# A two-layer attention and MLP training step: five wq chunks kept, w1's place lent to other loads, w2's chunks closed one by one

## The chip, the core and the metric

The kernel runs on one core of one Trainium2 chip. The metric is the device time of one execution in microseconds (us). Every matrix of weights is bf16 and far larger than what the core can keep, so it is moved in chunks of about 1 MB from HBM into the core's memory; results go back the same way.

## The reference

The forward pass is attention, MLP, attention, MLP on one token, with the same weights in both layers, and then the gradients of everything with respect to one given output gradient.

```python
def _A_ref(x, k_cache, v_cache, wq, wo):          # D=1024, 32 heads of 128, 4 kv heads, window W=4096
    q = (x @ wq).reshape(B, Sq, Hq, Dh) ...
    scores = jnp.einsum("bhqd,bhkd->bhqk", q, k) * (Dh ** -0.5)
    o = jnp.einsum("bhqk,bhkd->bhqd", _softmax(scores, axis=-1), v)
    return o... @ wo
def _B_ref(x, w1, b1, w2):                        # F=3584
    h = jnp.einsum("bsd,df->bsf", x, w1) + b1
    act = h * jnp.tanh(softplus(h))
    return jnp.einsum("bsf,fd->bsd", act, w2)
x = x + _A_ref(_layernorm(x), ...); x = x + _B_ref(_layernorm(x), ...)   # twice
...
_out, _vjp = jax.vjp(_f, A_x, A_k_cache, A_v_cache, A_wq, A_wo, B_w1, B_b1, B_w2)
return (_out0, *_vjp(grad_out))
```

The gradients of the two caches are as large as the caches (32768 rows, of which 4096 are in the window); all rows outside the window are zeros that must be written: 58.7 MB.

## The kernel before, in words

**The places in memory.** KT and VS hold the K and V windows of the four kv heads. W1 holds the whole of w1 (8 rows of chunks of 3584 columns). `ring_t` has 8 slots of 4096 columns; chunks of wq (8), wo (8) and w2 (7) pass through them. A chunk of wq, wo or w2 is 1 MB, one of w1 896 KB.

**The order of loads.** `Ring` (L38) holds a list of wanted loads, written out once at the start (L251 to L270): K into four ring slots, wq, V, two chunks of w2, wo, w1, the other five of w2, then for layer 1 wq, wo, and for the backward pass wq, w2, wo, wq again. `pump` (L51) issues from the head of the list on SP's queue as long as a slot is free; `release` (L77) frees a slot and pumps. Since this is done while the program is written down, the order of SP's queue is fixed; on the chip each load waits for the last reader or writer of its slot, and for the load eight places before it on the queue. SP also carries small moves of rows inside the core (L733, L737, L957, L792, L987) and the stores of the weights' gradients (L967, L972).

**Kept chunks.** `KEEP_Q = (6, 7)`: these wq chunks of layer 0 stay in their slots for layer 1, and six are loaded again. `KEEP_Q2 = (5, 6, 7)`: these stay after the backward pass of layer 1's attention (there already transposed in place, which `turned_q` remembers) for that of layer 0, and five are loaded again.

**Zero stores.** `zeros(n, after)` (L240) issues n stores of 1 MB of zeros on POOL's queue behind a one-element copy that waits for `after`. The 56 stores are dealt out over the milestones of the computation.

**The stages.** Forward: K transposes (L561), q (L473), scores, softmax, o, wo (L553), w1 (L601), w2 (`mlp_out`, L649). Since the output gradient is given, the product of w2's rows with it (da1) is made in the forward pass of layer 0, while w2 is in memory. `rows_chunk` (L447) does this: of a chunk's four row blocks two are dotted on VectorE (`rowdot`), and two are transposed on TensorE, copied back over the chunk by ScalarE and multiplied (`turned`, L427). The multiplication lags two blocks behind the transposes (`later`, `behind`), and the slot is released when it is done. For the last w2 chunk of layer 0 this is put off to `last_da` (L710), which attention of layer 1 calls ahead of its q. Backward: layer 1's MLP (`dn_b1`), layer 1's attention (`attn_bwd`, a loop over wo's chunks, scores, a loop over wq's chunks), layer 0's MLP (L1077 to L1081, forward product of layer 1's w2 and da0 together, then `dn_b0`), layer 0's attention. Last come the gradients of the weights and caches as outer products (L989 on), evacuated by ScalarE and VectorE into staging slots and stored. The staging slots are, in this order of taking, VS, KT, the ring and three slots at the end of W1.

Of the kernel before, what the change touches and what calls it, by code (L numbers as in the profile page):

```python
# [10 lines left out]
BF16 = mybir.dt.bfloat16  # L11
# [4 lines left out]
P = 128  # L16
HQ = 32
DH = 128
D = 1024
J = 4096  # L20
F = 3584
# [16 lines left out]
class Ring:  # L38
# [6 lines left out]
        self.pending = deque()  # L45
        self.where = {}

    def want(self, key, src, shape, own=None):
        self.pending.append((key, src, shape, own))

    def pump(self):  # L51
        while self.pending:
            key, src, shape, own = self.pending[0]
            if own is None:
                if not self.free:
                    return
                s = self.free.popleft()
                n = 1
                for k in shape[1:]:
                    n *= k  # L60
                dst = self.slots[s][:, 0:n]
                if len(shape) == 3:
                    dst = dst.rearrange("p (a b) -> p a b", a=shape[1])
                self.where[key] = (s, dst)
            else:
                dst = own
            self.pending.popleft()
            self.nc.sync.dma_start(dst, src)

# [6 lines left out]

    def release(self, key):  # L77
        s, _ = self.where.pop(key)
        self.free.append(s)
        self.pump()  # L80


# [1 line left out]
def kernel(  # L84
# [128 lines left out]
    def kv_src(cache, g):  # L213
        return cache[0, g, ZR:, :].rearrange("(p t) d -> p t d", p=P)
# [2 lines left out]
        for t in ts:  # L217
            ring.want(("q", k, t), wq_v[:, t, :], [P, J])

    def want_o(k, cs=range(8)):  # L220
        for c in cs:
            ring.want(("o", k, c), wo_v[:, c], [P, 4, D])

    def want_2(k, cs=range(7)):
        for c in cs:
# [22 lines left out]
                nc.gpsimd.dma_start(dst, zt[:])  # L248


    KEEP_Q = (6, 7)  # L251
    KEEP_Q2 = (5, 6, 7)
    EARLY_2 = (0, 1)
    for g in range(G):
        ring.want(("K", g), kv_src(A_k_cache, g), [P, TS, P])
    want_q(0)
    for g in range(G):
        ring.want(("V", g), kv_src(A_v_cache, g), None, own=VS[:, g])
    want_2(0, EARLY_2)
    want_o(0)  # L260
    for t in range(TD):
        ring.want(("1", t), w1_v[:, t, :], None, own=W1[:, t, :])
    want_2(0, [c for c in range(7) if c not in EARLY_2])
    want_q(1, [t for t in range(8) if t not in KEEP_Q])
    want_o(1)
# [161 lines left out]
    def turned(w, n, mv, eng=None, block=None):  # L427

        b = big().bitcast(BF16)
        for i in range(n):  # L430
            nc.tensor.transpose(b[:, i * P:(i + 1) * P], block(w, i) if block else w[:, i * P:(i + 1) * P], ident_bf[:])  # L431
        evac(w, b[:, 0:n * P], eng, cost=(0.69 * n / 8, n / 8))
        later(mv, True)
# [7 lines left out]
    def mv(w, n, out, rhs_of, last):  # L441
        for i in range(n):
            nc.tensor.matmul(out, lhsT=w[:, i * P:(i + 1) * P], rhs=rhs_of(i), start=fresh[0], stop=last and i == n - 1,  # L443
                             skip_group_check=True)
            fresh[0] = False

    def rows_chunk(ch, c, col, l, vec, dst, off, nr=2, eng="A"):  # L447

        for tt in range(4):
            r = 4 * c + tt  # L450
            if tt < nr:
                rowdot(ch[:, tt, :], [vec], D, dst[:, r:r + 1])
            else:
                w = ch[:, tt, :]
                turned(w, TD, lambda w=w, r=r: mv(w, TD, TP[:, off + r:off + r + 1], lambda i: col[:, i, l:l + 1], True), eng)

    def rows_join(dst, n, off):
        v = dst[:, 0:n].rearrange("p (a b) -> p a b", b=4)[:, :, 2:4]
# [136 lines left out]
    def mlp_fwd(l, x, st):  # L595
        name = f"B{l}"
        n32, rstd = ln_fwd(x, st, NB[:, :, l], name)
        h_ps = MV[:, 192:192 + TF]
        for t in range(TD):
            for fb in range(TF):  # L600
                nc.tensor.matmul(h_ps[:, fb:fb + 1], lhsT=f_block(W1[:, t], fb), rhs=NB[:, t, l:l + 1],  # L601
                                 start=(t == 0 and fb == 0), stop=(t == TD - 1), skip_group_check=True)
# [24 lines left out]
        if l == 0:  # L627
            V.tensor_tensor(out=AC[:, :, l], in0=h[:], in1=t_[:], op=ALU.mult)

        def deriv():  # L630

            mp, sg, s2 = col("mp"), col("sg"), col("s2")
            V.tensor_scalar(out=s2[:], in0=z[:], scalar1=1.0, scalar2=None, op0=ALU.add)
            V.reciprocal(s2[:], s2[:])
            V.tensor_tensor(out=sg[:], in0=m[:], in1=z[:], op=ALU.max)
            V.tensor_tensor(out=sg[:], in0=sg[:], in1=s2[:], op=ALU.mult)
            V.tensor_tensor(out=mp[:], in0=t_[:], in1=t_[:], op=ALU.mult)
            V.tensor_scalar(out=mp[:], in0=mp[:], scalar1=-1.0, scalar2=1.0, op0=ALU.mult, op1=ALU.add)
            V.tensor_tensor(out=mp[:], in0=mp[:], in1=h[:], op=ALU.mult)
            V.tensor_tensor(out=mp[:], in0=mp[:], in1=sg[:], op=ALU.mult)  # L640
            V.tensor_tensor(out=mp[:], in0=mp[:], in1=t_[:], op=ALU.add)
            return mp

        def act_late():
            V.tensor_tensor(out=AC[:, :, l], in0=h[:], in1=t_[:], op=ALU.mult)

        return dict(n32=n32, rstd=rstd, deriv=deriv, act_late=act_late)

    def mlp_out(l, ch, c, y_ps):  # L649
        for tt in range(4):  # L650
# [41 lines left out]
            early_da(2 * c + 1)  # L692

    x1, st1, sA0 = attn_fwd(0, x0, st0, True, wo_hook0)
    sB0 = mlp_fwd(0, x1, st1)
    mp0 = sB0["deriv"]()
    y_ps = MV[:, 256:256 + TD]
    mv_open()
    for c in range(7):
        ch = ring.get(("2", 0, c))  # L700
        mlp_out(0, ch, c, y_ps)
        if c in EARLY_2:
            ring.release(("2", 0, c))
        elif c < 6:
            rows_chunk(ch, c, GB, 1, gbc, da1, DA)
            later(lambda c=c: ring.release(("2", 0, c)))
    x2, st2 = residual(y_ps, x1, "B0")


# [223 lines left out]
                  dict(do=lambda c: conv(2), dp=dp3, dq=dq3, dn=dn3))  # L933


    W1S = W1[:].rearrange("p t f -> p (t f)")
    ROWS = W1S[:, 0:5120]
    NOFF = 1024
    rf = W1S[0:7, 5120:6144]
# [3 lines left out]
    DOST = W1S[:, 11008:11264]  # L943

    TWIN = W1S[:, 11264:16384]
    stage_free = deque(W1S[:, 16384 + i * SLOT:16384 + (i + 1) * SLOT] for i in range(3))
    rt_n = [0]

    def rowize(cols, n, base, off):
# [237 lines left out]
```

## Time and profile before

| what | us |
|---|---|
| median of 3 runs (lowest, highest) | 461.44 (459.64, 462.82) |
| span of the profiled execution | 460.6 |
| PE busy / PEld busy | 337.2 / 275.3 |
| DVE busy / ACT busy | 261.3 / 228.2 |
| DMA: loads and stores on SP's queue | 123.94 MB, 67.0% of 16 engines' span |
| DMA: zero stores on POOL's queue | 58.72 MB, 30.7% of 16 engines' span |

The page gives the span of one execution, from its first to its last instruction; it names no other time of its own, so the 0.84 us by which the median stands above it are taken as what lies around. PE is TensorE's matmuls, PEld its weight loads, DVE VectorE, ACT ScalarE, POOL GpSimd, SP the engine that issues most DMAs; a "q" behind a name (SPq) is the engine's sequencer. In the slices, each digit is the busy share of one fortieth of the span in tenths, and PEclk is TensorE's granted clock in tenths of full speed. A line of waits names who waited, for what, the us in total, the number of waits and the longest. A line of a timeline has start, duration, engine, line, operation, output and input, and in brackets the idle time of the engine ahead of it with what ended it.

### The profile page before, as it was taken

How to read it: one execution, taken by the hardware profiler on the slowest of the kernel's cores; microseconds unless marked ns; L12 is line 12 of the kernel's file. 1: busy time of each engine (PE TensorE's matmuls, PEld its weight loads, DVE VectorE, ACT ScalarE, POOL GpSimd, SP SyncE). 2: the span in 40 equal slices, each digit the busy share in tenths (PEclk: the TensorE clock that was granted, in tenths of full speed). 3: DMA queues.
4: the chain of work that ended last, by engine and by line, in shares of the span. 5: the costliest groups of instructions: out<-in, count | busy, mean ns of one | idle time of the engine just before them, and what ended most of it. 6: DMA issues, size and time to landing. Idle time of an engine off the chain costs nothing. (4 is left out here: it accounts for less than half of the span.)

```text
span 460.6 us, 14273 instructions
## 1 busy us (share of the span) xinstructions
PE 337.2 (73%) x6385; PEld 275.3 (60%) x6385; DVE 261.3 (57%) x517; ACT 228.2 (50%) x263; POOL 38.6 (8%) x85
## 2 busy tenths in 40 slices
PE   4836435597678788599879898897896876677950
PEld 3736435497668787599779898787791121112530
DVE  6505731383150149678428786475485987878860
ACT  2502001064035369378128573283267988778850
POOL 4000000000111320100210101102111000000000
PEclk9955555555555569799559855597595555555555
DMA  8999999999999999999999999979999999999995
GB/s 340 420 419 419 419 420 416 422 388 392 393 422 424 418 414 414 406 384 386 376 424 334 407 387 371 414 264 408 424 420 421 419 425 421 427 424 419 408 407 227
DMA packets 28379, 183.59 MB, mean 399 GB/s; under 512 B 3706, under 2 KB 3734, under 8 KB 9494
## 3 DMA queue, kind: packets, MB, share of 16 engines
q1 hardware_dynamic: 20162, 123.94, 67.0%
q0 software_dynamic: 8064, 58.72, 30.7%
q8 instruction: 50, 0.82, 0.7%
q14 instruction: 11, 0.09, 0.0%
q10 hardware_dynamic: 92, 0.02, 0.0%
HBM read 83.94 MB, written 98.62 MB: 396 GB/s over the span
## 5 line engine op out<-in xcount | busy, mean ns | idle before, releaser
L287 ACT COPY ring<-BIG 128x1024 bf16<-128x1024 bf16 x73 | 72.2, 1013 | 40.4 <-PE BIG L431 37.7
L431 PE MATMUL BIG<-ident_bf,ring 128*128 128x128 bf16 x872 | 80.0, 252 | 3.8 <-DMA ring<-in_A_wo_dram 2.0
L431 PEld LDWEIGHTS <-ring 128*128 128x128 bf16 x952 | 69.8, 114 | 5.2 <-DMA ring<-in_A_wo_dram 2.3
L995 PE MATMUL wide<-W 2*128 2x512 bf16 x228 | 48.5, 601 | 19.0 <-DVE ring L284 3.6
L408 DVE CUSTOM_DVE_ANT_0 junk<-ring,SC 128x1024 bf16<-128x1024 bf16 x38 | 46.2, 1216 | 4.5 <-DMA ring<-in_A_wo_dram 1.7
L995 PEld LDWEIGHTS <-W 2*128 2x128 bf16 x240 | 10.9, 103 | 54.5 <-issue 53.8
L443 PEld LDWEIGHTS <-ring 128*128 128x128 bf16 x1024 | 38.2, 100 | 4.6 <-ACT ring L287 4.4
L287 ACT COPY KT<-BIG 128x1024 bf16<-128x1024 bf16 x22 | 21.8, 1015 | 32.3 <-PE BIG L582 30.9
L287 ACT CAST ring<-wide 128x1024 bf16<-128x1024 f32 (+1 forms) x38 | 35.2, 998 | 4.9 <-PE wide L995 4.0
L284 DVE COPY ring<-BIG 128x1024 bf16<-128x1024 bf16 x36 | 24.8, 691 | 20.3 <-PE BIG L431 13.1
L284 DVE CAST ring<-wide 128x1024 bf16<-128x1024 f32 (+1 forms) x26 | 30.2, 1200 | 5.7 <-PE wide L995 5.2
L248 POOL DMA_DIRECT2D out_dram<-zt x56 | 29.6, 534 | 6.3 <-DMA out_dram<-zt 5.6
L553 PE MATMUL MV<-OC,ring 128*128 128x1 bf16 x512 | 16.6, 166 | 15.2 <-DMA ring<-in_A_wo_dram 12.6
L287 ACT COPY W<-BIG 128x1024 bf16<-128x1024 bf16 x20 | 18.9, 1151 | 15.7 <-PE BIG L766 15.7
L553 PEld LDWEIGHTS <-ring 128*128 128x128 bf16 x512 | 16.0, 106 | 16.0 <-DMA ring<-in_A_wo_dram 13.2
L284 DVE CAST VS<-wide 128x1024 bf16<-128x1024 f32 (+1 forms) x18 | 21.0, 1190 | 4.1 <-PE wide L995 3.1
L473 PE MATMUL MV<-NA,ring 128*128 128x1 bf16 x512 | 15.0, 165 | 10.9 <-DMA ring<-in_A_wq_dram 10.0
L601 PE MATMUL MV<-NB,W 128*128 128x1 bf16 x448 | 16.2, 172 | 9.2 <-DMA W<-in_B_w_dram 6.5
L408 DVE CUSTOM_DVE_ANT_0 junk<-ring,DSX 128x1024 bf16<-128x1024 bf16 x18 | 22.0, 1224 | 0.6
L601 PEld LDWEIGHTS <-W 128*128 128x128 bf16 x448 | 15.9, 118 | 9.8 <-DMA W<-in_B_w_dram 7.2
L1046 PE MATMUL wide<-W 32*128 32x256 bf16 x128 | 20.4, 403 | 1.4 <-ACT W L287 0.8
L473 PEld LDWEIGHTS <-ring 128*128 128x128 bf16 x512 | 14.3, 103 | 11.6 <-DMA ring<-in_A_wq_dram 10.6
(256 smaller groups left out, 539.1 us busy)
## 6 DMA issues: line engine op xcount, KB each, us to landing
out_dram<-zt POOLq DMA_DIRECT2D x56, 1024.0 KB, 12.7
ring<-in_A_wq_dram SPq DMA_DIRECT2D x27, 1024.0 KB
ring<-in_A_wo_dram SPq DMA_DIRECT2D x24, 1024.0 KB
ring<-in_B_w_dram SPq DMA_DIRECT2D x14, 1024.0 KB
out_dram<-ring SPq DMA_DIRECT2D x9, 1024.0 KB
W<-in_B_w_dram SPq DMA_DIRECT2D x8, 896.0 KB
ring<-in_A_k_cache_dram SPq DMA_DIRECT2D x4, 1024.0 KB
VS<-in_A_v_cache_dram SPq DMA_DIRECT2D x4, 1024.0 KB
```

Source lines behind the costliest of these rows:

```text
L248: nc.gpsimd.dma_start(dst, zt[:])
L284: nc.vector.tensor_copy(dst, src)
L287: nc.scalar.copy(dst, src)
L408: nc.vector.tensor_tensor_reduce(out=out, in0=a, in1=vec, scale=1.0, scalar=acc if i else 0.0, op0=ALU.mult, op1=ALU.add, accum_out=acc)
L431: nc.tensor.transpose(b[:, i * P:(i + 1) * P], block(w, i) if block else w[:, i * P:(i + 1) * P], ident_bf[:])
L443: nc.tensor.matmul(out, lhsT=w[:, i * P:(i + 1) * P], rhs=rhs_of(i), start=fresh[0], stop=last and i == n - 1, skip_group_check=True)
L473: nc.tensor.matmul(q_ps[:, h:h + 1], lhsT=ch[:, h * P:(h + 1) * P], rhs=NA[:, t, l:l + 1], start=(t == 0 and h == 0), stop=(t == TD - 1), ...
L553: nc.tensor.matmul(y_ps[:, dd:dd + 1], lhsT=ch[:, tt, dd * P:(dd + 1) * P], rhs=OC[:, h, l:l + 1], start=(h == 0 and dd == 0), stop=(h == ...
L601: nc.tensor.matmul(h_ps[:, fb:fb + 1], lhsT=f_block(W1[:, t], fb), rhs=NB[:, t, l:l + 1], start=(t == 0 and fb == 0), stop=(t == TD - 1), ...
L995: nc.tensor.matmul(b[:, 512 * i:512 * i + 512], lhsT=R[at:at + 2, lo:lo + P], rhs=R[at:at + 2, ro + 512 * i:ro + 512 * i + 512], start=Tru ...
L1046: nc.tensor.matmul(b[:, k * 256:(k + 1) * 256], lhsT=RT[32 * g:32 * g + 32, a, tp, :], rhs=YS[32 * g:32 * g + 32, :], start=True, stop=Tru ...
```

## The change

Five things are done together.

1. `KEEP_Q` and `KEEP_Q2` become (3, 4, 5, 6, 7): five wq chunks stay in the ring in both places; three loads fewer for layer 1, two fewer for the backward pass of layer 0.
2. W1 is cut into seven places of 4096 columns ("homes") while w1 is not there: K is loaded into the first four, wo's chunks 0 to 6 of layer 0 into all seven. A load of w1 is written down only when the wo chunks above its place are released (`over`).
3. `rows_closed` takes the place of `mlp_out` and `rows_chunk` in both w2 loops: per chunk it dots two blocks on VectorE, transposes the other two, does the forward product, then copies and multiplies, without lag, and releases the slot at once.
4. After `dn_b0` the three slots at the end of W1 are lent to the ring (`lend`), for wo chunks 3 to 5 and then two of wq; they come back as staging slots at the end, where they are now taken first.
5. One zero store is issued behind w1's last load; one less behind the backward wq loop's chunk 6.

```diff
+    def want(self, key, src, shape, own=None, over=()):
...
     def pump(self):
         while self.pending:
-            if own is None:
+            key, src, shape, own, over = self.pending[0]
+            if any(k in self.where for k in over):
+                return
+            if own is not None:
+                self.where[key] = (None, own)
...
+    def lend(self, slots):
+        self.free.extend(range(len(self.slots), len(self.slots) + len(slots)))
+        self.slots.extend(slots)
+        self.pump()
...
-    KEEP_Q = (6, 7)
-    KEEP_Q2 = (5, 6, 7)
+    KEEP_Q = (3, 4, 5, 6, 7)
+    KEEP_Q2 = (3, 4, 5, 6, 7)
+    homes = [W1S[:, i * SLOT:(i + 1) * SLOT] for i in range(7)]
     for g in range(G):
-        ring.want(("K", g), kv_src(A_k_cache, g), [P, TS, P])
+        ring.want(("K", g), kv_src(A_k_cache, g), None, own=homes[g].rearrange("p (t d) -> p t d", t=TS))
...
-    want_o(0)
+    want_o(0, homes=homes)
     for t in range(TD):
-        ring.want(("1", t), w1_v[:, t, :], None, own=W1[:, t, :])
+        under = [("o", 0, i) for i in range(7) if i * SLOT < (t + 1) * F and (i + 1) * SLOT > t * F]
+        ring.want(("1", t), w1_v[:, t, :], None, own=W1[:, t, :], over=under)
...
+    def rows_closed(ch, c, col, l, vec, dst, off, between):
+        rows = []
+        for tt in range(2):
+            rowdot(ch[:, tt, :], [vec], D, dst[:, 4 * c + tt:4 * c + tt + 1])
+        for tt in range(2, 4):
+            b = big().bitcast(BF16)
+            for i in range(TD):
+                nc.tensor.transpose(b[:, i * P:(i + 1) * P], ch[:, tt, i * P:(i + 1) * P], ident_bf[:])
+            rows.append(b)
+        between()
+        for tt in range(2, 4):
+            evac(ch[:, tt, :], rows[tt - 2][:, 0:D], "A")
+            r = off + 4 * c + tt
+            mv(ch[:, tt, :], TD, TP[:, r:r + 1], lambda i: col[:, i, l:l + 1], True)
...
     x1, st1, sA0 = attn_fwd(0, x0, st0, True, wo_hook0)
+    zeros(1, W1[:, TD - 1, 0:1])
...
-        mlp_out(0, ch, c, y_ps)
-        if c in EARLY_2:
+        if c in EARLY_2 or c == 6:
+            mlp_out(0, ch, c, y_ps)
+        else:
+            rows_closed(ch, c, GB, 1, gbc, da1, DA, lambda: mlp_out(0, ch, c, y_ps))
+        if c < 6:
             ring.release(("2", 0, c))
-        elif c < 6:
-            rows_chunk(ch, c, GB, 1, gbc, da1, DA)
-            later(lambda c=c: ring.release(("2", 0, c)))
...
-        mlp_out(1, ch, c, y_ps)
-        rows_chunk(ch, c, GB, 0, LB[0], da0, DA)
-        later(lambda c=c: ring.release(("2", 1, c)))
+        rows_closed(ch, c, GB, 0, LB[0], da0, DA, lambda: mlp_out(1, ch, c, y_ps))
+        ring.release(("2", 1, c))
...
     g1 = dn_b0(g2)
+    ring.lend(lent)
...
-            zeros(2 if t < 7 else 1, dnp[:, t:t + 1])
+            zeros(2 if t == 3 else 1, dnp[:, t:t + 1])
...
+    stage_free.extendleft(lent)
```

More of the change, by code (lines that the diff above doesn't have):

```diff
@@ L46, in __init__ @@
         self.where = {}
-    def want(self, key, src, shape, own=None):
-        self.pending.append((key, src, shape, own))
+    def want(self, key, src, shape, own=None, over=()):
+        self.pending.append((key, src, shape, own, over))
     def pump(self):
         while self.pending:
-            key, src, shape, own = self.pending[0]
-            if own is None:
+            key, src, shape, own, over = self.pending[0]
[3 more added lines that the diff above has]
+                self.where[key] = (None, own)
+                dst = own
+            else:
                 if not self.free:
@@ L64, in pump @@
                 self.where[key] = (s, dst)
-            else:
-                dst = own
             self.pending.popleft()
@@ L78, in release @@
         s, _ = self.where.pop(key)
-        self.free.append(s)
+        if s is not None:
+            self.free.append(s)
+        self.pump()
+    def lend(self, slots):
+        self.free.extend(range(len(self.slots), len(self.slots) + len(slots)))
+        self.slots.extend(slots)
         self.pump()
@@ L218, in want_q, with want_o @@
             ring.want(("q", k, t), wq_v[:, t, :], [P, J])
-    def want_o(k, cs=range(8)):
+    def want_o(k, cs=range(8), homes=()):
         for c in cs:
-            ring.want(("o", k, c), wo_v[:, c], [P, 4, D])
+            own = homes[c].rearrange("p (k d) -> p k d", k=4) if c < len(homes) else None
+            ring.want(("o", k, c), wo_v[:, c], [P, 4, D], own, [("K", c)] if own is not None else [])
     def want_2(k, cs=range(7)):
@@ L248, in zeros @@
                 nc.gpsimd.dma_start(dst, zt[:])
-    KEEP_Q = (6, 7)
-    KEEP_Q2 = (5, 6, 7)
+    KEEP_Q = (3, 4, 5, 6, 7)
+    KEEP_Q2 = (3, 4, 5, 6, 7)
     EARLY_2 = (0, 1)
+    W1S = W1[:].rearrange("p t f -> p (t f)")
+    homes = [W1S[:, i * SLOT:(i + 1) * SLOT] for i in range(7)]
     for g in range(G):
-        ring.want(("K", g), kv_src(A_k_cache, g), [P, TS, P])
+        ring.want(("K", g), kv_src(A_k_cache, g), None, own=homes[g].rearrange("p (t d) -> p t d", t=TS))
     want_q(0)
@@ L700 @@
         ch = ring.get(("2", 0, c))
-        mlp_out(0, ch, c, y_ps)
-        if c in EARLY_2:
+        if c in EARLY_2 or c == 6:
+            mlp_out(0, ch, c, y_ps)
+        else:
+            rows_closed(ch, c, GB, 1, gbc, da1, DA, lambda: mlp_out(0, ch, c, y_ps))
+        if c < 6:
             ring.release(("2", 0, c))
-        elif c < 6:
-            rows_chunk(ch, c, GB, 1, gbc, da1, DA)
-            later(lambda c=c: ring.release(("2", 0, c)))
     x2, st2 = residual(y_ps, x1, "B0")
@@ L933 @@
                   dict(do=lambda c: conv(2), dp=dp3, dq=dq3, dn=dn3))
-    W1S = W1[:].rearrange("p t f -> p (t f)")
     ROWS = W1S[:, 0:5120]
@@ L945 @@
     TWIN = W1S[:, 11264:16384]
-    stage_free = deque(W1S[:, 16384 + i * SLOT:16384 + (i + 1) * SLOT] for i in range(3))
+    lent = [W1S[:, 16384 + i * SLOT:16384 + (i + 1) * SLOT] for i in range(3)]
+    stage_free = deque()
     rt_n = [0]
```

## The prediction

> **What bounds the kernel now.** I read the slices first: are the DMA engines full, and what runs beside them?
>
> ```profile
> span 460.6 us, 14273 instructions
> ...
> PEclk9955555555555569799559855597595555555555
> DMA  8999999999999999999999999979999999999995
> ```
>
> The DMA engines are at nine tenths or more in 38 of 40 slices, so the bytes look like the bound. Second, the windows by stage and the waits of TensorE, which tell whether anybody waits for those bytes.
>
> ```profile
> 2.00:88.00 86.00, 46.10 (x1161) 42.78 (x1162) 32.69 (x76) 13.64 (x18) 4.15 (x4) 0.62 1.01 417
> 88.00:110.00 22.00, 17.67 (x391) 17.42 (x391) 16.70 (x49) 13.20 (x16) 0.00 (x0) 0.50 0.98 389
> ...
> 262.00:284.00 22.00, 20.59 (x427) 20.42 (x426) 16.68 (x32) 14.07 (x14) 0.87 (x3) 0.50 1.00 392
> ...
> 346.00:455.00 109.00, 73.39 (x402) 25.80 (x401) 79.55 (x80) 83.11 (x96) 1.30 (x4) 0.50 1.01 417
> ```
> ```profile
> PE MV L553 <- DMA ring<-in_A_wo_dram: 12.6, 8, 2.3
> PE MV L473 <- DMA ring<-in_A_wq_dram: 10.0, 7, 1.6
> PE MV L601 <- DMA W<-in_B_w_dram: 6.5, 6, 1.1
> ...
> PE BIG L431 <- DMA ring<-in_A_wo_dram: 2.0, 2, 1.4
> ```
>
> Columns of the windows: length, then PE, PEld, DVE, ACT, POOL busy, granted clock, DMA share, GB/s. Up to 88 us TensorE is idle half the time and waits for loads. From 88 to 345 us it is 75 to 94% busy and waits for loads 3 to 4 us in all; the zero stores of out_2 and out_3 (q0, 58.72 MB) fill the DMA engines there, and they wait for milestones of the computation. So there are two bounds: loads to 88 us, the computation to 345 us, and from 346 us on the stores (39.9 MB at 419 GB/s are 95.2 us), with ACT and DVE 76 and 73% busy beside them. What the change does to the middle part decides.
>
> Third, the timelines: what a load costs whose slot has just come free.
>
> ```profile
> 110.09 0.33 SPq L68 DMA_DIRECT2D ring<-in_A_wq_dram  x1
> ```
> ```profile
> 115.62 1.55 PE L473 MATMUL MV<-NA,ring 128*128 128x1 bf16 x52 [1.34 <-DMA ring<-in_A_wq_dram]
> ```
> ```profile
> 266.39 0.33 SPq L68 DMA_DIRECT2D ring<-in_B_w_dram  x1
> ```
> ```profile
> 275.06 1.22 DVE L408 CUSTOM_DVE_ANT_0 junk<-ring,SC 128x1024 bf16<-128x1024 bf16 x1 [1.58 <-DMA ring<-in_B_w_dram]
> ```
>
> From issue to first use: 5.5 us with no zero store about (110.09 to 115.62), 8.7 us with zero stores in flight (266.39 to 275.06; q0 has 96% of the DMA time from 262 to 269 us). In a full queue the same megabyte costs 2.5 us. These prices carry the sum.
>
> **Bytes.** Three wq loads fewer before layer 1, two fewer before the last use: 5.24 MB, at 419 GB/s 12.5 us of DMA time. SP issues five DMAs less (0.33 us each), which nobody waits for. On POOL one zero store with its one-element copy moves ahead of layer 1's QC copy; it waits for w1's last load (86.7 us), that copy runs at 119.7, so it costs nothing. These 12.5 us are worth something only where the path waits for DMA; after 88 us it hardly does.
>
> **Start to 88 us: nothing.** K goes to w1's place, so wq chunks 4 to 7 lose their wait for the K transposes (SP, L567, 10.8 us in four waits); the DMA share was 1.01 anyway. w1's loads now wait until TensorE has used the wo chunks above them: wo 5 is used up at 65.3 us, one us after w1's load 5 was issued (64.30). Some six loads of 2.2 to 2.5 us stand ahead of it, and they hide that us. If that cover were gone it would cost 1 us.
>
> **The forward w2 loop and q of layer 1 (90 to 119 us).** Five of eight ring slots now hold wq, so w2 and wq share three. Before, w2 chunks 2 to 5 stood in the queue behind w1. Now only chunk 2 does; 3 and 4 wait for the products of chunks 0 and 1 (91.2 and 92.1 us, the times of the last w2 load and the first wq load of before), 5 and 6 for the closing of 2 and 3.
> A closed chunk costs: 8 transposes 0.81, 0.24 to ACT's start, two ACT copies 1.93, then 0.37 for the last product: 3.35 us, where the lagged loop takes 2.99 (mlp_out at 97.46 and 100.45 us). The new zero store (after w1's last load, 86.7 us; first packets 4.2 us after issue, as at 119.81 to 124 us) shares the engines with chunks 3 and 4. So chunk 3 lands at about 97.5, is closed at 100.9, chunk 4 at 104.2, 5 at 107.6, and chunk 6's product starts at 107.6 instead of 103.43: 4.1 us late.
> Then wq: chunks 0 and 1 are loaded in time into the slots of 4 and 5, but chunk 2 needs chunk 6's slot, which comes free when last_da has ended (110.0 before, 114.1 now). It lands 5.5 us later, at 119.6, and TensorE, which takes wq in order, stands before it for 3.8 us with five kept chunks behind it. Six chunks of 0.88 us follow: 124.9 against 119.4. **Term 1: +5.6 us**, with ends 4.3 (the zero store in nobody's way) and 9 (8.7 us for chunk 2). I stay by the 5.5 us row since q0 is empty at 114 us. Queued behind on TensorE is all of attention. wo of layer 1 has 17 us until its first use and stays hidden.
>
> A page on this price: the Trainium skill's DMA: Bandwidth & Descriptors, section Anatomy of one DMA, fits a fixed 2.0 us plus the bytes at 436 GB/s. That is 4.4 us for such a load, an estimate from that page; the rows say 5.5 and 8.7. By it the whole sum below would be near 462.
>
> **The backward w2 loop (260 to 283 us).** Three slots again, not five. Seven chunks at 3.35 instead of 21.9 us in all: 23.5, so +1.6. Chunk 3's load waits for chunk 0's closing (263.7 on before's clock), just as three zero stores (issued at 260.24) start; by the 8.7 us row it lands at 272.4, needed at 270.7: 1.7 us. Chunks 4 to 6 then come as they are needed. **Term 2: +3.4** (1.6 to 6).
>
> **The last wo loop (293 to 317 us).** Before, loads 5 to 7 waited for a ring slot at 301.4 us and TensorE waited 2.0 us for them (L431). Now 3 to 5 go into the lent slots after w1's last reader, behind rowize on SP (294.6), with two zero stores of 292.7 us beside them. At half rate they land at about 301, 306 and 309.7; chunks 4 and 5 are needed at 304.7 and 306.8: 2.9 us of waits, and the old 2.0 go. **Term 3: +1.2** (-2.0 to +3).
>
> **The last wq loop (330 to 347 us).** Five kept chunks instead of three arrive turned: six transposed groups less. TensorE saves 0.65 us for each, 3.9 us; DVE, which ends this stage, saves only its one copy and gaps: five row products of 1.27 after 338.5 end at 344.9, not 346.5. **Term 4: -1.7** (to -3.9).
>
> **The tail.** The stores begin 8.5 us late (361.5). What is won: zero stores took 69% of 353 to 363 us, 6.9 us. Now 12 instead of 13 are issued from 319 us on, beside fewer loads: from 333.6 us on, 12 of 2.5 us, to 363.6, that is 2.1 us past the first store. So 4.8 us come back. That backlog also fed the engines across gaps in SP's issues (none from 377.3 to 382.7 us): 2.1 instead of 6.9 us of it leave up to 3.3 us idle; I take half, 1.6.
> The sum on the profiled execution: 460.6 + 5.6 + 3.4 + 1.2 - 1.7 - 4.8 + 1.6 = 465.9. The page names only the span; the median of the runs shown, 461.44, is 0.84 above it. With that: 467.
>
> **Rivals.** *Bytes decide (faster):* the loads in reused slots land before their chunk is needed, so that terms 1 and 2 vanish and the 12.5 us come off: 449; the computation's own end (445.3 us, then the last stores, some 9 us) less 1.7 and 2.0 allows 451. For it: the full DMA slices. Against it: chunk 2 of wq cannot be asked for before last_da's end. It decides if term 1 is under 1 us.
> *Quick landing:* every reused slot is refilled in 5.5 us, no zero store is in the way: terms 4.5, 1.6, 0, -1.7, and the tail gives back what is left: 461 to 463, 462.
> *The clock falls:* the granted clock is 1.00 from 299 to 316 us and 0.50 after the waits at 310.9 and 314.4 us. With waits of 1.6 and 1.3 us at chunks 4 and 5 it could fall ten us earlier: a transposed group then takes 1.07 instead of 0.65 us (rows of 264 and 302 us). Nine groups are 3.8 us; with half the groups of the wq loop 6: 473. Against it: dense transposes ahead of each loop have raised the clock so far.
> The Trainium skill's TensorE: Matmul & The Clock Gate, Part 1, says that an idle window of about 3.4 us halves the clock. The trace agrees in sign, not in the limit: 0.50 stands from 90 to 110 us with TensorE 80% busy.
>
> **How the numbers follow.** Forecast 0.52, with its own range 460 to 473 (three in five of it above 466); quick landing 0.20; bytes 0.15; clock 0.13. One per cent, about what a measurement here can tell from no change, is 456.8 to 466.1. Faster: bytes and a quarter of quick landing, 0.20. Slower: three fifths of the forecast and the clock, 0.45. Same: 0.35. The range of 455 to 474 leaves out most of the bytes case and some of the clock's.
>
> **What would show it.** The product of the last forward w2 chunk starts at 107 to 108 us; a TensorE wait of 3 to 5 us on wq (L473's line) near 119; attention of layer 1 some 5 us late; the DMA share under 0.85 from 88 to 120 us and again near 259 to 264 us; a chunk pitch of 3.3 to 3.5 us in both w2 loops; fewer waits at the wo loop's end, more in its middle; first store near 361 us; q0 done within 3 us of it. It is wrong if wq chunk 2 lands with chunk 1, or if the lagged loops were not what paced TensorE.

## The result, and the profile after

The changed kernel takes 479.76 us (median of 4 runs, 479.37 to 480.85) against 461.0 for the kernel before beside it (4 runs): 1.041 times as long, interval 1.038 to 1.044. It moves 5.26 MB less (178.33 in place of 183.59 MB) and is 18.8 us slower. The forecast was 467, with 455 to 474 as its range. The profiled execution has a span of 477.8 us. The profiled execution of one experiment further down, the first that moves zero stores behind the backward w2 loop, was a disturbed one, slower than its three others, so its time is given as the median of those three, and only times inside its loops are read from its profile.

The slices of the page after; the DMA row has two hollows now, at 84 to 119 us and at 263 to 311 us (a slice is 11.9 us):

```profile
span 477.8 us, 14145 instructions
...
PEclk9955555555555559799759755577766555555555
DMA  8999999875999999999999695899999999899998
```

Around both w2 loops the DMA engines are a quarter to a third idle, as two windows of the kernel after show (columns as in the prediction). The start is as it was (a DMA share of 1.00 from 2 to 88 us), and the tail is nearly full again (0.97 from 366 to 475 us):

```profile
88.00:120.00 32.00, 20.77 (x450) 19.60 (x449) 16.94 (x50) 12.91 (x16) 0.09 (x1) 0.50 0.68 244
...
275.00:304.00 29.00, 19.19 (x379) 18.13 (x378) 12.55 (x23) 11.56 (x12) 0.54 (x2) 0.50 0.73 259
```

So in these stretches it is not the number of bytes that takes the time. TensorE's waits in the backward w2 loop say what does, first before (260 to 284 us), then after (262 to 304 us):

```profile
PE TP L443 <- ACT ring L287: 0.7, 1, 0.7
```
```profile
PE TP L457 <- ACT ring L301: 10.5, 14, 1.2
```

No load is in that list after. TensorE stands twice in each of seven chunks and waits for ScalarE's copy; from 88 to 130 us, over the forward loop and `last_da`, it does so ten times, for 7.8 us. ScalarE in turn waits for L683, which is the forward product. Its lines before, where it waits for the transposes (L431) and the copies of one chunk start 2.99 us behind those of the last, then after:

```profile
268.12 2.03 ACT L287 COPY ring<-BIG 128x1024 bf16<-128x1024 bf16 x2 [0.95 <-PE BIG L431]
271.11 2.03 ACT L287 COPY ring<-BIG 128x1024 bf16<-128x1024 bf16 x2 [0.95 <-PE BIG L431]
```

```profile
271.64 1.93 ACT L301 COPY ring<-BIG 128x1024 bf16<-128x1024 bf16 x2 [4.25 <-PE MV L683]
276.38 1.93 ACT L301 COPY ring<-BIG 128x1024 bf16<-128x1024 bf16 x2 [2.81 <-PE MV L683]
```

One chunk of the closed loop on TensorE, after:

```profile
273.86 1.87 PE L479 MATMUL BIG<-ident_bf,ring 128*128 128x128 bf16 x16
275.52 1.04 PE L683 MATMUL MV<-AC,ring 128*128 128x1 bf16 x32
277.45 0.38 PE L457 MATMUL TP<-GB,ring 128*128 128x1 bf16 x8 [0.89 <-ACT ring L301]
278.36 0.38 PE L457 MATMUL TP<-GB,ring 128*128 128x1 bf16 x8 [0.54 <-ACT ring L301]
```

`rows_closed` copies the transposed block in place, over the block from which it came. The forward product, put between the transposes and the copies, still reads that block, so the copy has to wait for the product: it starts at 276.38, 2.52 us after the chunk's first transpose (1.66 for the transposes, 0.86 into the product), not 1.05. The two copies take 1.93, the last product 0.29 more; the next chunk begins at 278.60. The pitch, from one chunk's first transpose to the next one's, is 4.74 us here and 4.74 to 5.06 from the second chunk on. In the lagged loop of before, the product of a chunk stands ahead of its transposes, and a copy waits for nothing but them.

In layer 1's q, wq chunk 2 is issued when `last_da` has ended and TensorE stands before it (SP's and TensorE's timelines, after):

```profile
117.70 0.33 SPq L71 DMA_DIRECT2D ring<-in_A_wq_dram  x1
```
```profile
122.49 1.65 PE L503 MATMUL MV<-NA,ring 128*128 128x1 bf16 x56 [3.16 <-DMA ring<-in_A_wq_dram]
```

Where the time came, as the delay against before at seven points, read from the timelines of VectorE (us, each profile from its own start; the columns to the right are the experiments below). Each column is one execution: "split" and "split, kept first", whose forward loops are the same, differ by 1.0 us at x_B, and the one of "layer 1 only" is the fastest of its ten (460.64 us; median 462.53):

| point | before at | after | part 3 alone | split | lagged | split, kept first | layer 1 only | stores behind wo |
|---|---|---|---|---|---|---|---|---|
| end of forward w2 loop (x_B) | 104.5 | +7.6 | +7.5 | +3.6 | +4.5 | +4.6 | +3.7 | +3.7 |
| q of layer 1 | 119.4 | +10.2 | +7.5 | +6.5 | +7.7 | +4.7 | +3.6 | +3.9 |
| end of layer 1's attention (x_A) | 152.2 | +9.2 | +8.4 | +4.5 | +7.2 | +2.0 | +0.8 | +1.0 |
| start of backward w2 loop (GB) | 260.0 | +8.8 | +8.1 | +8.0 | +7.7 | +2.6 | +1.0 | +1.8 |
| its end (da) | 282.6 | +20.3 | +19.6 | +14.7 | +15.7 | +9.1 | +1.6 | +5.1 |
| end of last wo loop (da) | 317.7 | +21.7 | +18.1 | +15.2 | +16.0 | +11.5 | +0.3 | +5.4 |
| last milestone (g0b) | 349.2 | +20.9 | +20.6 | +13.9 | +15.6 | +11.2 | +1.2 | +5.9 |
| span | 460.6 | +17.2 | +19.3 | +10.2 | +12.0 | +7.5 | -1.7 | +5.1 |

### The profile page after: what moved, and what is told of

It reads as the page before. It is cut to its first block, busy times and chain, and to the rows that moved or that the text cites. A ratio compares the mean times of both kernels' runs of the same rounds, so it can differ in the third digit from the quotient of the medians.

```text
span 477.8 us, 14145 instructions
## 1 busy us (share of the span) xinstructions
PE 339.5 (71%) x6337; PEld 274.7 (57%) x6337; DVE 260.1 (54%) x515; ACT 224.1 (47%) x259; POOL 38.8 (8%) x86
## 2 busy tenths in 40 slices
DMA packets 27658, 178.33 MB, mean 373 GB/s; under 512 B 3626, under 2 KB 3654, under 8 KB 9414
## 5 line engine op out<-in xcount | busy, mean ns | idle before, releaser
L301 ACT COPY ring<-BIG 128x1024 bf16<-128x1024 bf16 x62 | 60.6, 1014 | 55.0 <-PE MV L683 21.4
L422 DVE CUSTOM_DVE_ANT_0 junk<-ring,SC 128x1024 bf16<-128x1024 bf16 x34 | 41.3, 1216 | 9.9 <-DMA ring<-in_B_w_dram 8.7
L445 PE MATMUL BIG<-ident_bf,ring 128*128 128x128 bf16 x544 | 45.4, 240 | 1.6 <-ACT W L301 1.1
L457 PEld LDWEIGHTS <-ring 128*128 128x128 bf16 x896 | 30.9, 99 | 25.2 <-ACT ring L301 22.4
L445 PEld LDWEIGHTS <-ring 128*128 128x128 bf16 x600 | 41.8, 110 | 2.6 <-issue 2.2
L298 DVE CAST ring<-wide 128x1024 bf16<-128x1024 f32 (+1 forms) x29 | 33.8, 1201 | 9.0 <-PE wide L1026 6.3
L301 ACT COPY W<-BIG 128x1024 bf16<-128x1024 bf16 x28 | 26.7, 1112 | 19.2 <-PE BIG L797 15.1
L301 ACT CAST ring<-wide 128x1024 bf16<-128x1024 f32 (+1 forms) x35 | 33.1, 1000 | 4.3 <-PE wide L1026 2.7
L298 DVE COPY ring<-BIG 128x1024 bf16<-128x1024 bf16 x28 | 19.4, 691 | 17.8 <-PE BIG L445 10.8
L503 PEld LDWEIGHTS <-ring 128*128 128x128 bf16 x512 | 14.3, 103 | 13.7 <-DMA ring<-in_A_wq_dram 12.0
L301 ACT CAST KT<-wide 128x1024 bf16<-128x1024 f32 x20 | 20.2, 1022 | 4.2 <-PE wide L1026 3.1
L457 PE MATMUL TP<-GB,ring 128*128 128x1 bf16 x192 | 8.9, 168 | 18.3 <-ACT ring L301 18.3
```

What stands on the lines that cost most here:

```text
L298: nc.vector.tensor_copy(dst, src)
L301: nc.scalar.copy(dst, src)
L422: nc.vector.tensor_tensor_reduce(out=out, in0=a, in1=vec, scale=1.0, scalar=acc if i else 0.0, op0=ALU.mult, op1=ALU.add, accum_out=acc)
L503: nc.tensor.matmul(q_ps[:, h:h + 1], lhsT=ch[:, h * P:(h + 1) * P], rhs=NA[:, t, l:l + 1], start=(t == 0 and h == 0), stop=(t == TD - 1), ...
```

## The experiments

Two theories. **A**: the in-place copy waits for the forward product, and this order, not any load, sets the loops' pitch. **B**, the prediction's: three slots for w2 and wq, refilled late, cost the time. The first four kernels ran beside the same runs of before (459.99 us).

**Part 3 alone.** The kernel before, with nothing of the change but the closed loops (the backward one is shown; the forward one is changed alike):

```diff
-        mlp_out(1, ch, c, y_ps)
-        rows_chunk(ch, c, GB, 0, LB[0], da0, DA)
-        later(lambda c=c: ring.release(("2", 1, c)))
+        rows_closed(ch, c, GB, 0, LB[0], da0, DA, lambda: mlp_out(1, ch, c, y_ps))
+        ring.release(("2", 1, c))
```

> The kernel before with part 3 of the change alone: both w2 loops close their chunks one by one (seven backward, four forward); the ring, its five free slots, the kept chunks and all loads stay as before. Theory A: ScalarE's copy writes the transposed block back over the block that the forward product still has to read, so it waits for the whole product, and the pitch of a chunk is 4.78 us for reasons of order alone. Then the pitch is 4.7 to 4.8 us here too, the backward loop is about 11 us longer than before, the forward one about 7, and the time is 13 to 18 us over before (what the tail gives back is the rest). Theory B, the prediction's: the closed chunk itself costs 3.35 us and the refilling of three shared slots is the loss. Then, with five slots, the pitch is 3.35, the loops are 1.6 and 1.4 us longer, and the time is within 4 us of before.

Measured: 480.39 us, 1.044 times before (1.039 to 1.048). The forward loop is 7.5 us longer and the backward one 11.5, with five slots and every load as before. ScalarE's lines in this kernel (L669 is its forward product):

```profile
271.23 1.93 ACT L287 COPY ring<-BIG 128x1024 bf16<-128x1024 bf16 x2 [4.49 <-PE MV L669]
275.97 1.01 ACT L287 COPY ring<-BIG 128x1024 bf16<-128x1024 bf16 x1 [2.81 <-PE MV L669]
```

The pitch is 4.74 us to the hundredth. A is right: the order alone, with none of B's late loads, is enough for the whole loss. A's total was too low (13 to 18): the tail gave back only 1.3 us (20.6 late at the last milestone, 19.3 at the end), perhaps since all bytes were still to be moved. Part 3 alone costs as much as the whole change.

**The product split.** The changed kernel; the product is cut into its four blocks, so that each copy waits for the product of its own block alone:

```diff
                 nc.tensor.transpose(b[:, i * P:(i + 1) * P], ch[:, tt, i * P:(i + 1) * P], ident_bf[:])
             rows.append(b)
-        between()
+            part(tt)
+        part(0)
+        part(1)
```

> The changed kernel, with the forward product cut into its four blocks and each put where ScalarE's copy need not wait for another's: transposes of block 2, product of block 2, transposes of 3, product of 3, then products of 0 and 1, then copies' products. The same instructions, no load changed. Theory A (the copy waits for the whole product): the pitch falls from 4.78 to about 3.5 us, the forward loop is 4 to 5 us and the backward one 7 to 8 us shorter than in the changed kernel, TensorE now waits for one or two w2 loads for 1 to 3 us; the time is 8 to 11 us under the changed kernel, that is 8 to 11 us over before. Theory B (the refilling of three slots sets the loops): the pitch stays at 4.7 us, each us won in a chunk comes back as a wait for the next load, and the time stays within 3 us of the changed kernel.

Measured: 473.57 us, 1.028 times before (1.025 to 1.031), 6 under the changed kernel. One chunk on TensorE, and the wait that appears in its place at chunk 3:

```profile
271.70 1.01 PE L479 MATMUL BIG<-ident_bf,ring 128*128 128x128 bf16 x8
272.51 0.40 PE L686 MATMUL MV<-AC,ring 128*128 128x1 bf16 x8
272.77 1.01 PE L479 MATMUL BIG<-ident_bf,ring 128*128 128x128 bf16 x8
273.57 0.82 PE L686 MATMUL MV<-AC,ring 128*128 128x1 bf16 x24
274.26 0.35 PE L457 MATMUL TP<-GB,ring 128*128 128x1 bf16 x8
275.07 0.38 PE L457 MATMUL TP<-GB,ring 128*128 128x1 bf16 x8 [0.46 <-ACT ring L301]
275.31 1.01 PE L479 MATMUL BIG<-ident_bf,ring 128*128 128x128 bf16 x8
...
282.29 1.03 PE L479 MATMUL BIG<-ident_bf,ring 128*128 128x128 bf16 x8 [3.23 <-DMA ring<-in_B_w_dram]
```

The same instructions in another order: 3.61 us a chunk (271.70 to 275.31) in place of 4.74. ScalarE's copy still stands behind the product of its own block: it starts at 272.94, 1.24 us after the chunk's first transpose and not 1.05. The forward loop wins 4.1 us as expected, the backward one 4.9 instead of 7 to 8, because a load is now waited for: B comes true as soon as A is gone. The time (8 to 11 under was expected) misses for two reasons. The wait, 3.2 us, is a little above the 1 to 3 expected, and between layer 1's w1 products and the backward loop this execution lost 3.5 us again (+4.5 at x_A, +8.0 at GB). Its trace shows 2.6 of them: TensorE's waits marked "issue" are 4.5 us in that stretch, 1.9 before, and at most 2.7 in the other kernels of the table. The cause of these waits is open (last section).

**The lagged loops under three slots.** The changed kernel with part 3 undone, so all of the change but the closed loops.

> The changed kernel with part 3 undone: the w2 loops are the lagged ones of before, everything else is as changed. Theory A: the loops run at 3.0 to 3.1 us a chunk until a slot is missing; since a slot is released two blocks later than in the closed loop, TensorE waits for loads once or twice in each loop, 3 to 5 us in the forward and 3 to 8 us in the backward loop, which leaves 5 to 12 us under the changed kernel. Theory B: with the slots released still later, the refilling costs more than the 4.78 us pitch, and the time is that of the changed kernel or above it.

Measured: 474.68 us, 1.032 times before (1.028 to 1.035), 5 under the changed kernel: A's lower end. TensorE's waits for w2 (13.0 us, none of them in the list of before), and the refill of chunk 3, which SP issued at 273.61:

```profile
PE MV L683 <- DMA ring<-in_B_w_dram: 13.0, 7, 6.3
```
```profile
281.94 1.01 PE L683 MATMUL MV<-AC,ring 128*128 128x1 bf16 x32 [6.32 <-DMA ring<-in_B_w_dram]
```

So the two halves do not add up. Part 3 without the rest costs 20.4 us, the rest without part 3 costs 14.7, both together 18.8: a loop of 4.74 us a chunk is slow enough for three slots to be refilled beneath it. The backward loop takes 30.7 us here (GB to da), 29.3 with the split closed loop, which by the program releases a slot sooner, 34.2 with the change as it was, 22.6 before.

**Kept chunks first.** The split product, and layer 1's q takes the kept wq chunks 3 to 7 first:

```diff
-        for t in range(TD):
+        ts = list(range(TD)) if first else [*KEEP_Q, *(t for t in range(TD) if t not in KEEP_Q)]
+        for t in ts:
```

> The split product of the run before, and besides, in layer 1's q loop the five kept wq chunks are used first and the three loaded ones (0, 1, 2) last. The prediction's reading of the q loop: TensorE stands 3.2 us before chunk 2 with five kept chunks behind it. Then the wait goes, and the time is 3 to 4 us under the run before. The rival: the q loop is paced by something else (the products of the MLP ahead of it, or the two waits of 1.7 and 2.2 us without a load in them that stand in the same stretch), and less than 1 us comes back.

Measured: 468.98 us, 1.018 times before (1.013 to 1.022). The wait for wq is gone; one wait is left in q, and it has no load in it:

```profile
122.78 1.31 PE L506 MATMUL MV<-NA,ring 128*128 128x1 bf16 x44 [2.56 <-issue]
```

From x_B to the end of q it takes 15.1 us, 17.8 in the run before: 2.7 us won, a little under the wait of 3.2. The medians differ by 4.6 us, the two profiled executions by 2.7 at their end: q accounts for the second, and the rest is not followed (the four executions here lie between 466.4 and 470.1). Chunk 3 of the backward w2 loop is still waited for: issued at 266.55, used at 276.90 by TensorE (3.20 us of waiting).

**The forward half alone.** The kernel of kept chunks first, with the backward half of before (`KEEP_Q2 = (5, 6, 7)`, lagged loop, no lent slots).

> Forward half as in the last kernel (five chunks kept for layer 1, the places of w1 lent, product split, kept chunks first); backward half as before the change: three chunks kept, five free slots, the lagged loop, no lent slots behind dn_b0. Theory: the backward half's loss (6.5 us between its start and the end of the w2 loop, 2.3 in the wo loop) is the price of three slots for w2. Then it goes, layer 0's last milestone (g0) is 2 to 3 us behind before instead of 11, and of the three loads saved only the one zero store that moved forward comes back in the tail: 458 to 462 us, the same as before. Rival, bytes decide: 3.1 MB less to move take 7 us off wherever they are saved: 453 to 455. Rival, the loss has its root in the forward half: g0 stays more than 6 us late, 464 or more.

Measured: 462.53 us, 1.002 times before (1.000 to 1.005): no difference, half a us above the theory's range. Nearly all of the remaining loss was the backward half's: 9.0 us over before with it, 1.1 without. Which of its three parts (kept chunks, closed loop, lent slots) costs how much was not taken apart further. 3.14 MB are saved and nothing is won. Where they went is seen in the windows from 85 to 115 us, before and in this kernel:

```profile
85.00:110.00 25.00, 19.40 (x438) 19.01 (x437) 16.86 (x49) 13.20 (x16) 0.00 (x0) 0.50 0.99 393
110.00:115.00 5.00, 4.28 (x161) 4.19 (x158) 0.17 (x1) 0.00 (x0) 0.00 (x0) 0.50 1.01 423
```
```profile
85.00:110.00 25.00, 18.71 (x410) 17.99 (x408) 13.91 (x43) 10.07 (x13) 0.86 (x2) 0.50 0.85 316
110.00:115.00 5.00, 2.95 (x81) 2.61 (x79) 3.14 (x8) 3.22 (x4) 0.00 (x0) 0.50 0.49 151
```

The DMA engines are idle there for 25 x 0.14 + 5 x 0.52 = 6.1 us more, of the 7.5 us that 3.14 MB take at 419 GB/s. The saved loads became a hole at the place where they were saved.

**Zero stores into the hole, at 115 us** (`zeros(2, ...)` behind `last_da`, two fewer in the last backward loop), and the same with four chunks kept.

> The kernel before this one, and two more zero stores taken from the last backward loop (its chunks 6 and 7) and issued after layer 1's first products (last_da), where the DMA engines stand idle for 3 us since three loads are gone. Theory: saved bytes are worth something only if other transfers take their place there; two stores are 5 us of DMA time, the tail begins with that much less in the queue, and the time is 3 to 5 us under the run before. Rival: the tail is paced by the evacuations of ScalarE and VectorE, or wq's last chunk and wo are delayed by the stores by as much: within 1 us of the run before.

> The kernel with the zero stores moved forward, but four wq chunks kept for layer 1, not five: w2 and wq share four slots and one more load is needed. Theory: three slots are what delays the forward w2 loop and wq's last chunk; with four, w2 chunk 3 stands in the queue early and layer 1's q ends 1.5 to 3 us earlier; the load of 1 MB costs 2.5 us of DMA time: the time is 0 to 2 us under the run with five. Rival: the loop's length is the split closed chunk's own (3.6 us against 3.0), the q ends as late as with five, and the time is 1 to 2.5 us above.

Measured: 463.94 us, 1.006 (1.004 to 1.008), no better than without: the rival. The stores start after the hole and meet layer 1's wo loads; x_A comes 5.0 us later than in the run before, as much as two stores take:

```profile
PE MV L586 <- DMA ring<-in_A_wo_dram: 2.9, 1, 2.9
```

With four chunks kept: 462.33 us, 1.004 (1.001 to 1.006). q is 1.5 us earlier and the time 1.6 under the one with five, as the theory had it, though the two intervals overlap.

**Zero stores into the hole, at 105 us** (behind w2 chunk 5's row product), with a control in the kernel before and a version with four chunks kept:

```diff
+        if c == 5:
+            zeros(2, da1[:, 20:21])
...
-        if t in (3, 6, 7):
-            zeros(2 if t == 3 else 1, dnp[:, t:t + 1])
+        if t == 3:
+            zeros(2, dnp[:, t:t + 1])
```

> The kernel with the change's forward half only (median 462.5), and two zero stores taken from the last backward loop and issued behind the row product of w2 chunk 5, at 105 us, so that their packets start at about 109 us and fill the stretch from 110 to 115 us, where the DMA engines were 37% busy. The last run issued them at 115 us and they took 5 us from layer 1's wo loads. Theory: a saved byte is worth its time only if another transfer is moved exactly into the hole; these two are nearly free where they now stand and 5 us of the tail go: 457 to 460 us, 1.5 to 5 under the same kernel without them. Rival: the hole is only the waiting time of wq's last load and of w2's last ones, which the stores prolong: layer 1's q 2 to 5 us later, and the time the same as without them or above.

> A control: the kernel before with the same two zero stores moved from the last backward loop to the same place. There the DMA engines are full at 100 to 120 us. Theory: what the tail wins, the loads of wq and wo lose: within 3 us of before on either side, and layer 1's attention (wo loop) 3 to 5 us later. Rival: the tail's backlog of zero stores is a loss by itself wherever there is room before it: 3 to 5 us under before.

> As the first of these three, but four wq chunks kept for layer 1 instead of five: one slot more for w2, one load more. Theory (slots): layer 1's q is 0 to 1 us earlier, the extra load costs up to 2.5 us of DMA time where there is little hole left: 0 to 2 us above the one with five. Rival: with the fourth slot the loop loses less than the load costs, 1 to 2 us under it.

Measured, against before at 460.88: five kept 459.87 (0.997; 0.994 to 0.999), control 458.91 (0.996; 0.993 to 0.999), four kept 458.82 (0.995; 0.993 to 0.997). In the first the hole is filled (a DMA share of 0.99 from 110 to 115 us) and q no later (+3.3 against +3.6), as the theory says. But x_A comes 2.0 us later than without the stores (155.0 against 153.0 us), with no wait for a load on the way but with 2.0 us more of waits marked "issue", and another hole opens where the tail had drawn on the two stores (its share was 1.01 without the move):

```profile
350.00:360.00 10.00, 7.83 (x35) 2.06 (x33) 5.65 (x10) 8.80 (x14) 0.00 (x0) 0.50 0.80 327
```

The control is 2 us under before, within the theory's 3, but with its interval under 1, and that takes from the theory its sole claim: moving two stores is worth as much without a hole. There they delay q by 5.1 us, but 2.9 are won back by x_A and nearly all of the rest by the end of the last wo loop (+0.3); which waits took it up was not followed. The one with four kept fell as its rival had it, by 1 us, with intervals that overlap. So these three versions lie 0.3 to 0.5 per cent under the kernel before, which their intervals only just clear, and what they show of the hole by itself is little: the kept chunks add nothing measurable to the control.

**The refill without zero stores ahead of it.** The kernel with kept chunks first; the three zero stores at the start of the backward w2 loop (`zeros(3, g2)`) are issued at its end, and in a second kernel after the last wo loop.

> The kernel of the split product and kept chunks first, with the three zero stores at the start of the backward w2 loop issued behind the loop instead (five there in place of two). Theory of the prediction, in its place once the product no longer covers it: the refill of w2 chunk 3 took 10.3 us from issue to use because three zero stores stood in front. Then it takes 5 to 6 us, TensorE's 3.2 us wait for it goes to under 0.5, and the w2 loop ends 3 us earlier; the time falls by 1 to 3 us, since the stores meet wo's loads later on. Rival: the refill is slow by itself, the wait stays over 2 us, and the time is the same or above.

> As the run that moved three zero stores from the start of the backward w2 loop to its end, but they are issued after the last wo loop (seven there in place of four), where no load of wo can meet them. In the first try the refill of w2 chunk 3 was in time (4.9 us from issue to first use in place of 10.4) and the loop ended 2.8 us earlier, but the stores met wo's loads and TensorE waited 9.7 us for them. Theory: it was the meeting, and the refill alone is worth its 3 us: the w2 loop 2.8 us shorter, the wo loop no longer than with the stores ahead of the loop, layer 0's last milestone 2 to 5 us earlier (the wait of 2.4 us for wo goes too); of this the tail gives back some, since the three stores now lie closer to it: 465 to 469 us, against 469. Rival, bytes: the DMA engines stand idle in the w2 and wo loops for as long as the stores would have taken, 7.5 us, and the tail is that much longer: 470 to 474 us.

The DMA queues in two windows of the kernel with the stores ahead, 266.5 to 270 us and 270 to 274 us (packets, MB, share of the 16 engines; q1 has the loads). The load of chunk 3 is issued at 266.55 and has no packet in the first:

```profile
q0 software_dynamic: 203, 1.41, 103.9%
```
```profile
q0 software_dynamic: 99, 0.68, 57.6%
q1 hardware_dynamic: 82, 0.67, 39.6%
```

The first use of chunk 3 on VectorE in that kernel, and in the second kernel without the stores, where it is issued at 265.85:

```profile
276.98 1.22 DVE L422 CUSTOM_DVE_ANT_0 junk<-ring,SC 128x1024 bf16<-128x1024 bf16 x1 [5.94 <-DMA ring<-in_B_w_dram]
```
```profile
270.64 1.22 DVE L422 CUSTOM_DVE_ANT_0 junk<-ring,SC 128x1024 bf16<-128x1024 bf16 x1 [0.46 <-DMA ring<-in_B_w_dram]
```

10.4 us from issue to use against 4.8 (4.9 in the first kernel, 271.04 to 275.93): the prediction's row was right that the queue ahead decides. TensorE waits for w2 no more, and the loop takes 26.0 us (26.4 in the first), not 29.2. In the first kernel the stores then met wo's loads (TensorE waited 9.7 us for one in the profiled execution), and the time is 473.44 us, 1.027 times before (1.022 to 1.032), not the gain expected. In the second it is 467.61 us, 1.018 (1.014 to 1.021): in the range expected, and by its interval the same as with the stores ahead. Of the 5.3 us by which its profile is ahead of that kernel's at the last milestone, 2.4 are left at the end. The w2 loop's windows show the hole that stayed (262 to 292 us, stores ahead, then stores behind wo):

```profile
262.00:292.00 30.00, 22.14 (x456) 21.39 (x456) 18.08 (x34) 14.07 (x14) 1.77 (x4) 0.54 0.85 315
```
```profile
262.00:292.00 30.00, 25.82 (x570) 25.03 (x570) 20.58 (x40) 14.43 (x15) 1.25 (x3) 0.52 0.73 239
```

Not tried: a copy into a place of its own, which would take away what makes it wait.

## Why the prediction was wrong, step by step

- **The closed chunk, the step that failed.** The prediction put it as "8 transposes 0.81, 0.24 to ACT's start, two ACT copies 1.93, then 0.37 for the last product: 3.35 us". It named the copies' wait for the transposes and left out their wait for the product whose source they overwrite. Measured 4.74. Of the 1.75 us over the lagged loop's 2.99, the product's place is 1.13 (4.74 less 3.61 with the product split) and the closing itself 0.62 (3.61 less 2.99), where 0.36 was given. The 0.26 between these two is as long as the product of the copy's own block (272.51 to 272.77), which stands ahead of the copy in the split loop too; so all but the wait for the product was sized well. The question could have been put to the change itself: which instruction still reads the tile that a copy writes?
- **Term 1, +5.6: measured +10.2 at q.** x_B came 7.6 us late, not 4.1, by the pitch. The 3.8 us before wq chunk 2 were 3.2 (1.3 of a load wait of before went), since it came 4.8 us after its issue and not 5.5; the reason given was right, as the experiment that takes the kept chunks first removed the wait. The rest is a wait of 1.7 us without a load in it, where before had 0.9. The new zero store's first packet came 1.3 us after its issue (87.41 to 88.66), not 4.2.
- **Term 2, +3.4: measured +11.5** (20.3 less 8.8). Seven chunks at 1.75 are 12.3, less at the first chunk, which took 4.39 us at a higher clock (0.80 from 262 to 275 us, 0.50 from there to 304). The 1.7 us for chunk 3's refill did not show, because the slow loop covered it; with the loop repaired it was 3.2.
- **Term 3, +1.2: measured +1.4, by luck.** It was to be load waits of 2.9 us in place of 2.0. TensorE waited for wo once, 1.7 us (up to 326.61), so the waits got shorter. What got worse is the granted clock: 0.50 from 327.9 to 334.7 us, in the midst of the loop, where before had 1.00 from 299 to 316 us, up to near its end. That this made the 1.4 us was not tested.
- **Term 4, -1.7: measured -1.8** (22.1 at the end of layer 0's q gradient to 20.3 at the end of the wq loop). **Start to 88 us, nothing: measured +0.1** at the end of w1. **The tail, -3.2: measured -3.1** (20.3 at the end of the wq loop to 17.2 at the end of the span). These stand as worked out, though each alone was not put to a test.
- **Its sums.** By their own figures term 1 is 5.5 (124.9 less 119.4), term 2 is 3.3 and term 3 is 0.9, half a us less in all; and 37 slices of before are at nine tenths, not 38. Nothing hangs on it.
- **The rivals.** *Bytes decide* asked for term 1 under 1 us; term 1 was ten, and the DMA engines stood idle in the hollows. *Quick landing* had the refill right for an empty queue (4.8 us, where the prediction took 5.5), but it was not the bound. The Trainium skill's DMA: Bandwidth & Descriptors, section Anatomy of one DMA, gives 4.4 us for such a load, an estimate from a fit that the page makes for DMAs issued by GpSimd; the trace of these loads on SP's queue agrees within 0.5 us where no store stands ahead (117.70 to 122.49), and not where three do (10.4). *The clock falls* came true in small, in the last wo loop: 0.78 (313 to 339 us) against 0.84 (293 to 318 us), within the 1.4 us of term 3; the rest of the loss lies elsewhere.
- **The forecast's last sentence** named two ways to be wrong: wq chunk 2 landing early, or the lagged loops not pacing TensorE. It was neither; they did, and what took their place was slower than read. The range's upper end, 474, had room for refills and the clock, and no term for a chunk's order at all.

## What to carry to other kernels

Before an in-place copy is costed, list who still reads the place: whatever is put between the read and the copy lies on the copy's path, and moving a reader is enough to win it back (4.74 to 3.61 us a chunk here, with the same instructions). Two losses that cover each other do not add: 20.4 and 14.7 us gave 18.8 together, so the second shows only when the first is repaired, and each part has to be run without the other. A load saved in a stage that waits for slots or order left a hole here (6.1 of its 7.5 us), not time.

## What the runs showed of the hardware

**Behind a burst of zero stores a load does not share, it stands.** Issued at 266.55, with three zero stores issued at 262.9 to 264.7, it had no packet before 271.5 us while q0 took all 16 engines (103.9% in the fence above), then some 40%. In the second kernel without the stores ahead the first packet came 1.0 us after issue (265.85 to 266.8). The Trainium skill's DMA: Bandwidth & Descriptors, section Queues, rings and completion order, has each engine take turns, packet by packet, between the queues it has work for; the 4.9 us from issue to first packet do not agree with that, unless the load's work reached the engines late, which no trace here shows.

**TensorE's waits marked "issue" end just behind a packet of the queue called instruction.** Such waits of 0.8 to 2.6 us wander from line to line between runs. In before, two of them, and that queue's one 16 KB packet from 142.9 to 144 us; from 149.4 to 150.4 us it has one more, and none between 144 and 149:

```profile
145.28 0.64 PE L553 MATMUL MV<-OC,ring 128*128 128x1 bf16 x19 [1.21 <-issue]
...
151.75 0.41 PE L553 MATMUL MV<-OC,ring 128*128 128x1 bf16 x10 [1.00 <-issue]
```
```profile
q8 instruction: 1, 0.02, 5.5%
```

The packets end at 143.93 and 150.39, 1.35 and 1.36 us ahead of the end of the waits. All five such waits of 0.8 us or more that before has between 88 and 345 us end 1.26 to 1.36 us behind the end of such a packet. It fits that TensorE waits for its next instructions there. It was seen, not tested.
